# Gated linear attention and a channel mixer on one core: batch 0 by token slot, more transposes by DMA, and a new written-out order

## The chip, the cores and the metric

The kernel runs on one core of a Trainium2 chip. A core has a matrix engine (PE, with its weight load PEld), a vector engine (DVE), an activation engine (ACT), a general engine (POOL), and a queue engine (SP) that issues transfers; ACT can issue transfers too. All of them run their own list of instructions strictly in order and meet at semaphores. Sixteen DMA engines move the data. The metric is device time in microseconds (us), the median of several runs.

## The reference, cut to what matters

```
state = zeros(B, H, D, D)                       # B=4, H=8, D=48, S=768 tokens
for t in range(S):
    state = alpha[t][:, None] * state + outer(k[t], v[t])
    y[t] = q[t] @ state
x  = y as (B, S, H*D)                            # H*D = 384
h  = relu(x^T @ w_tok1) @ w_tok2                 # 768 -> 256 -> 768, over tokens
u  = x + h^T
out = u + relu(u @ w_ch1) @ w_ch2                # 384 -> 1536 -> 384, over channels
```

The recurrence is computed in chunks: cumulative products of alpha (as exponentials of cumulative sums of logarithms) scale k and q, a masked product of scaled q and k gives the part within a chunk, and a carried state gives the rest. Everything in and out is float32; the matrix work is in bf16.

## The kernel before, in words

**Attention.** Twelve units n = 0 to 11, three to a batch of 256 tokens each. A unit loads alpha, k, q and v (`ld_at`, `ld_kt`, `ld_qt`, `ld_vt`, 384 KB each, L534). A partition holds two neighbouring tokens, its two slots. In the wide units, 0 to 2 (batch 0), logarithms (`ln`), cumulative sums by matrix product (`cumw`, L608) and exponentials (`E`, `IE`, `Et`) cover both slots; the others fold the two slots first (`P`, `k0a`, `q0r`). `kk` and `qq` scale k and q (L640), and eight transposes on PE for each (`trk`, `trq`) with an eviction (`evk`, `evq`) turn them; from unit 6 on, DMA transposes issued by SP do it (`dk`, `dq`, L664) with a reorder of q behind (`pq`). `G0`, `G1` are the products within a half of the unit, `mask0`, `mask1` the masked evictions on DVE (L700). Six half-tile copies (`vs0`, `vs1`, `ka`, `kb`, `kc`) regroup v and k so that `K`, the update of the state, runs on full 128-row tiles. The states follow as an add on DVE (`sa`) and a multiply (`sm`). `y0`, `y1` with `ia`, `ib` give the outputs and `x0`, `x1` evict them.

**Mixer.** For each batch b: `t1_b` (token matrix 1, L787), its rectifying evictions `ht_b`, `t2_b` (L792), `u_b` (add on DVE, L796, six tiles), the transposes of u, `c1_b` (channel matrix 1, 24 groups of three 128x384 products, L811) with evictions `rt_b` on ACT or DVE, `c2_b` (six rows of four groups, L816), `o_b` (add on DVE, L820) and a store `st_b` (L574). The transposes of u are `up` on PE with evictions `ut` in batches 0 and 1, and `ux`, a DMA transpose on SP, in batches 2 and 3. PE's results lie in eight PSUM banks. The output tiles `o` are three: an `o` waits until the store of the earlier content of its tile has landed.

**Order.** Nothing is scheduled on the chip or by the compiler. `ORDER` lists every step with its engine's letter (t PE, s ACT, v DVE, g POOL, y SP), `BUFS` the buffer of every tile; a search outside the kernel wrote both. Steps of one engine run in the listed order. Loads and weight pieces are issued by SP and ACT. [...] `f1`, `f3` steps are fillers: PE products of zeros that keep it busy at the start.

Of the kernel before, what the change touches and what calls it, by code (L numbers as in the profile page):

```python
# [110 lines left out]
WIDE = (0, 1, 2)  # L111

# [3 lines left out]
def build(g):  # L116
# [8 lines left out]
    def filler(nm, bank):  # L125
        return [P.op(f"f{z}_{nm}", {"PE": pe([512] * z)["PE"], "NONE": (0.0, 0.0)}, -100, writes=[bank],
                     emit=lambda e, z=z: g.fill(bank, z)) for z in (1, 3)]

    def attention(n):
# [8 lines left out]
        def fill(nm, bank):  # L138
            return filler(f"{nm}{n}", bank) if n < NB else []

        at, kt, qt, vt = V("in"), V("in"), V("in"), V("in")
# [4 lines left out]
        la, E, IE = V("la"), V("E"), V("IE")
        pkk, pkq, vb = V("pkk"), V("pkq"), V("vb")
        k_in, q_in = [ld["kt"]], [ld["qt"]]
        if n in WIDE:
# [4 lines left out]
            e1 = O("E", act(768), 4, writes=[E], reads=[cb], preds=[cum], emit=lambda e: g.exps(E, cb, 1.0))
            et = O("Et", act(16), 6, writes=[E], reads=[cb], preds=[cum], emit=lambda e: g.exptot(E, cb))
            e2 = O("IE", act(768), 3, writes=[IE], reads=[cb], preds=[cum], emit=lambda e: g.exps(IE, cb, -1.0))
        else:
# [8 lines left out]
            e1 = et = O("E", act(400), 4, writes=[E], reads=[cb], preds=[cum], emit=lambda e: g.expE(E, cb))  # L166
            e2 = O("IE", act(384), 4, writes=[IE], reads=[cb], preds=[cum], emit=lambda e: g.expIE(IE, cb))
# [5 lines left out]
        kk = O("kk", either(dve(768), pool_tt(768)), 5, writes=[pkk], reads=[kt, IE], port=True, preds=k_in + [e2],  # L173
               emit=lambda e: g.scaled(e, pkk, kt, IE, wide))
        qq = O("qq", either(dve(768), pool_tt(768)), 5, writes=[pkq], reads=[qt, E], port=True, preds=q_in + [e1],
               emit=lambda e: g.scaled(e, pkq, qt, E, wide))
# [3 lines left out]
        if n < NX:  # L180
            bk, bq = V("one"), V("one")
            trk = O("trk", pe([128] * 8), 8, writes=[bk], reads=[pkk], preds=[kk] + fill("trk", bk),
                    emit=lambda e: g.trw(bk, pkk))
            evk = O("evk", either(dve(1024, True), act(1024)), 9, writes=[tpk], reads=[bk], preds=[trk],
                    emit=lambda e: g.trwev(e, tpk, bk))
            trq = O("trq", pe([128] * 8), 8, writes=[bq], reads=[pkq], preds=[qq] + fill("trq", bq),
                    emit=lambda e: g.trw(bq, pkq))
            evq = O("evq", either(dve(1024 * 1.065), act(1024 * 1.34)), 9, writes=[tpq], reads=[bq], preds=[trq],
                    emit=lambda e: g.qev(e, tpq, g.bank(bq).bitcast(BF16)))
        else:  # L190
            evk = O("dk", {"SP": (1240.0, 1240.0)}, 9, writes=[tpk], reads=[pkk], preds=[kk],
                    emit=lambda e: g.xbar(tpk, pkk), dma=("x", 1400.0, 1180.0, 480.0))
            tqx = V("tpk")
            xq = O("dq", {"SP": (1240.0, 1240.0)}, 9, writes=[tqx], reads=[pkq], preds=[qq],
                   emit=lambda e: g.xbar(tqx, pkq), dma=("x", 1400.0, 1180.0, 480.0))
            evq = O("pq", either(dve(1024), act(1024 * 1.35, True), {"POOL": (1100.0, 1140.0)}), 9.5, port=True, writes=[tpq], reads=[tqx], preds=[xq],
                    emit=lambda e: g.qev(e, tpq, g.t(tqx)))
        gtm = V("gtm")
        masks = []
        for hf in range(2):  # L200
            gp = V("pair")
            G = O(f"G{hf}_", pe([128] * 4), 10 + hf, writes=[gp], reads=[tpk, tpq], preds=[evk, evq] + fill(f"G{hf}", gp),
                  emit=lambda e, hf=hf, gp=gp: g.gmm(gp, tpk, tpq, hf), mode="G")
            masks.append(O(f"mask{hf}_", dve(1024), 12 + hf, writes=[gtm], reads=[gp], preds=[G],
                           emit=lambda e, hf=hf, gp=gp: g.mask(gtm, gp, hf)))
        nst = 2 if k < NB - 1 else 1
        kp = V("pair")
# [4 lines left out]
        vsw = lambda hf, preds: shift(f"vs{hf}_", 10, [vb], [vt], preds, lambda e: g.vswap(e, vb, vt, hf))  # L212
        turned = n >= KFN
        if turned:
            vs = [vsw(hf, [vc]) for hf in range(2)]
            kx, kp_in = None, [kk, vc, vs[0]]
            if nst == 2:
                kx = V("kt")
                ka = shift("ka", 9, [kx], [pkk], [kk], lambda e: g.kturn(e, kx, pkk, 0))
                kb = shift("kb", 9, [kx], [pkk], [kk], lambda e: g.kturn(e, kx, pkk, 1))  # L220
                kp_in += [ka, kb, vs[1]]
            kc = shift("kc", 9, [pkk], [], [kk, trk if n < NX else evk] + ([ka] if nst == 2 else []),
# [4 lines left out]
        else:  # L227
            KO = O("K", {"PE": (276.0 if nst == 2 else 140.0, 420.0)}, 9.5, writes=[kp], reads=[pkk, vb],
                   preds=[kk, vc] + fill("K", kp) + ([prev_s[1]] if prev_s and k > 0 and n > NB else []),
                   emit=lambda e: g.kmm(kp, pkk, vb, nst), mode="G")  # L230
            vs = [vsw(hf, [KO, vc]) for hf in range(2)]
        before = prev_s if k > 0 else None
        states = [before]
        for hf in range(nst):
            s_, sp = V("ss"), states[-1]
            if sp is None:
                so = O(f"s{hf}_", dve(384), 10, writes=[s_], reads=[kp, E], preds=[KO, et],
                       emit=lambda e, s_=s_, hf=hf: g.sfirst(s_, kp, E, hf, wide, turned))
            else:
                t_ = V("tmp")  # L240
                ad = O(f"sa{hf}_", dve(384), 10 + hf, writes=[t_], reads=[kp, sp[0]], preds=[KO, sp[1]],
                       emit=lambda e, t_=t_, hf=hf, s0=sp[0]: g.sadd(t_, kp, s0, hf, turned))
                so = O(f"sm{hf}_", either(dve(384), pool_tt(384)), 11 + hf, writes=[s_], reads=[t_, E], port=True,
                       preds=[ad, et], emit=lambda e, s_=s_, t_=t_, hf=hf: g.smul(e, s_, t_, E, hf, wide))
            states.append((s_, so))
        for hf, st in enumerate(states[:2]):
            yp, x = V("one"), V("x")
            held = []
            if st:
                held.append(O(f"i{'ab'[hf]}", pe([96] * 4), 13, writes=[yp], reads=[tpq, st[0]],  # L250
                              preds=[evq, st[1]] + (fill("y", yp) if hf else []),
                              emit=lambda e, hf=hf, st=st, yp=yp: g.inter(yp, tpq, st[0], hf)))
            yo = O(f"y{hf}_", pe([48] * 8), 14, writes=[yp], reads=[gtm, vb],
                   preds=[masks[hf], vs[hf]] + held,
                   emit=lambda e, hf=hf, yp=yp, st=st: g.ymm(yp, gtm, vb, hf, not st))
# [619 lines left out]
```

## Time and profile before

| | |
|---|---|
| runs | 167.32, 166.66, 166.67 us; median 166.67 |
| profiled execution | span 165.0 us from first to last instruction; its whole time isn't given on the page, the median lies 1.67 us above its span |
| busy | PE 156.2 us (95%), DVE 121.2 (73%), ACT 96.2 (58%), POOL 68.7 (42%) |
| granted PE clock | 1.000 over the span |
| first product of c1_0 / last PE product | starts 37.34 us / ends 161.97 us |

A row of a group reads: line, engine, operation, output<-input, shapes, count, then busy us and mean ns of one, then the idle time of the engine ahead of it and what ended that. A row of the timeline reads: start us, length us, engine, line, operation, count. A row of the stretches reads: from:to, length, and for each engine its busy us with the count, then the granted clock, the busy share of the DMA engines and GB/s.

### The profile page before, as it was taken

The numbers are of one execution on the slowest core, as the hardware profiler recorded it, in microseconds if no ns is written. First come the engines' busy times: TensorE is split into PE (matmuls) and PEld (weight loads), VectorE is DVE, ScalarE is ACT, GpSimd is POOL, SyncE is SP. The second block draws the span as 40 slices with busy tenths as digits, with TensorE's granted clock in tenths as the row PEclk, the third lists the DMA queues.
The fourth block names the chain that finished last, engine by engine and source line by source line (L and its number), as shares of the span: only waits on it lengthen the run. The fifth ranks groups of instructions, "written<-read, shape, count | busy, mean of one in ns | idle before, by whom it ended". The sixth has DMA issues, their size and how long they took to land.

```text
span 165.0 us, 4235 instructions
## 1 busy us (share of the span) xinstructions
PE 156.2 (95%) x1683; PEld 99.2 (60%) x1683; DVE 121.2 (73%) x210; ACT 96.2 (58%) x186; POOL 68.7 (42%) x84
## 2 busy tenths in 40 slices
PE   7969769999999999999999999999999999999992
PEld 2435446666666766576666666666666656656662
DVE  4098989989898898798878999989492455524422
ACT  3599987998877837939887746913614001514110
POOL 4025659497217475792388528973300000000000
PEclk9999999999999999999999999999999999999999
DMA  4999999999999999999989996898001136200213
GB/s 121 324 325 325 337 347 316 365 327 352 371 335 347 326 315 226 307 252 264 136 198 255 211 250 120 219 181 183 0 4 48 49 75 157 105 0 0 99 72 119
DMA packets 74531, 34.48 MB, mean 209 GB/s; under 512 B 67984, under 2 KB 73488, under 8 KB 74512
## 3 DMA queue, kind: packets, MB, share of 16 engines
q1 hardware_dynamic: 50576, 23.30, 55.2%
q10 hardware_dynamic: 23936, 10.91, 24.3%
q8 instruction: 13, 0.21, 0.5%
q14 instruction: 6, 0.05, 0.1%
HBM read 25.17 MB, written 4.72 MB: 181 GB/s over the span
## 4 chain that ended last, share of the span: by engine, by line
PE 83%; DMA 4%; SPq 3%; POOL 2%; issue 2%; ACT 2%; DVE 1%; POOLq 0%; DVEq 0%
PE ps L816 29%; PE ps L811 29%; PE ps L593 14%; PE ps L792 5%; DMA in<-in_v_dram 4%; PE ps L787 4%; SPq L534 3%; PE ps L654 1%; PE ps L803 1%; POOL pkk L642 1%; DVE gtm L700 1%; POOL vb L685 1%; ACT x L684 1%; POOL ss L753 1%; ACT E L626 0%
## 5 line engine op out<-in xcount | busy, mean ns | idle before, releaser
L816 PE MATMUL ps<-wc,rt 128*128 128x384 bf16 (+1 forms) x300 | 54.7, 320 | 0.0
L811 PE MATMUL ps<-ut,wc 128*128 128x384 bf16 x288 | 51.3, 326 | 0.0
L782 ACT ACTIVATE rt<-ps 128x384 bf16<-128x384 f32 x54 | 24.4, 490 | 35.4 <-PE ps L811 34.7
L811 PEld LDWEIGHTS <-wc 128*128 128x128 bf16 x288 | 27.1, 98 | 16.7
L816 PEld LDWEIGHTS <-rt 128*128 128x128 bf16 x300 | 27.5, 98 | 15.9
L700 DVE TENSOR_TENSOR gtm<-ps,mk 128x1024 bf16<-128x1024 f32 x24 | 28.7, 1219 | 4.8 <-PE ps L593 3.4
L784 DVE TENSOR_SCALAR rt<-ps 128x384 bf16<-128x384 f32 x42 | 21.7, 551 | 9.2 <-PE ps L811 9.2
L820 DVE TENSOR_TENSOR o<-ps,u 128x384 f32<-128x384 f32 (+1 forms) x25 | 13.1, 537 | 10.0 <-PE ps L816 9.1
L685 POOL CAST vb<-in 64x384 bf16<-64x384 f32 (+1 forms) x18 | 10.9, 608 | 15.2 <-DVE pkk L642 8.9
L593 PE MATMUL ps<-zs 128*128 128x512 bf16 x38 | 12.7, 452 | 2.9 <-DVE zs L496 1.1
L684 ACT CAST x<-ps 128x384 bf16<-128x384 f32 x17 | 7.8, 477 | 10.7 <-PE ps L593 10.5
L796 DVE TENSOR_TENSOR u<-ps,x 128x384 bf16<-128x384 f32 x24 | 11.8, 550 | 3.0 <-PE ps L792 3.0
L642 DVE TENSOR_TENSOR pkq<-in,E 128x768 bf16<-128x768 f32 x8 | 7.6, 954 | 5.4 <-ACT E L626 5.2
L787 PE MATMUL ps<-x,wt 128*128 128x384 bf16 x48 | 11.1, 325 | 0.5 <-DVE gtm L700 0.4
L684 ACT CAST vb<-in 64x384 bf16<-64x384 f32 (+1 forms) x18 | 11.1, 618 | 0.7 <-DMA in<-in_v_dram 0.2
L642 POOL TENSOR_TENSOR pkk<-in,IE 128x768 bf16<-128x768 f32 x5 | 9.1, 1816 | 4.9 <-DVE pkk L685 3.2
L753 POOL TENSOR_TENSOR ss<-tmp,E 128x384 bf16<-128x384 f32 x11 | 9.2, 833 | 3.2 <-DVE tmp L750 2.9
L750 DVE TENSOR_TENSOR tmp<-ps,ss 128x384 f32<-128x384 f32 x16 | 8.8, 552 | 1.0 <-PE ps L593 0.5
L792 PE MATMUL ps<-ht,wt 128*128 128x384 bf16 x48 | 9.5, 326 | 0.0
L593 PEld LDWEIGHTS <-gtm 128*128 128x128 bf16 x192 | 7.4, 96 | 2.7 <-DVE gtm L700 0.9
L593 PEld LDWEIGHTS <-tpk 48*64 48x64 bf16 x384 | 6.1, 106 | 4.9 <-issue 4.3
L593 PE MATMUL ps<-vb,gtm 128*128 128x48 bf16 x192 | 8.6, 183 | 0.4 <-DVE gtm L700 0.4
(91 smaller groups left out, 216.6 us busy)
## 6 DMA issues: line engine op xcount, KB each, us to landing
in<-in_moe_w_ch_dram SPq DMA_DIRECT2D x10, 384.0 KB, 6.2
in<-in_alpha_dram SPq DMA_DIRECT2D x9, 384.0 KB, 6.8
out_dram<-o SPq DMA_DIRECT2D x16, 192.0 KB, 2.5
in<-in_q_dram SPq DMA_DIRECT2D x7, 384.0 KB, 6.3
in<-in_v_dram ACTq DMA_DIRECT2D x7, 384.0 KB, 6.0
in<-in_k_dram ACTq DMA_DIRECT2D x6, 384.0 KB, 5.7
in<-in_k_dram SPq DMA_DIRECT2D x6, 384.0 KB, 6.2
in<-in_v_dram SPq DMA_DIRECT2D x5, 384.0 KB, 7.2
```

The costliest lines, as they stand in the source:

```text
L593: return self.pe.matmul(out, lhsT=lhsT, rhs=rhs, start=start, stop=stop, skip_group_check=True)
L642: self.shared(self.eng[e].tensor_tensor(self.t(dst)[:, :, :, 0:D], self.t(src).rearrange("p h s d -> p s h d"), bass.AP(tensor=f.tensor, o ...
L684: return self.act.copy(d, s)
L685: return self.shared(self.eng[e].tensor_copy(d, s))
L700: self.nc.vector.tensor_tensor(self.t(gtm)[:, hf, :, :], self.pair(gp).rearrange("p a (j t) -> p (a j) t", t=128), bass.AP(tensor=m.tensor ...
L782: self.act.activation(d, s, AF.Relu)
L784: self.nc.vector.tensor_scalar_max(d, s, 0.0)
L787: self.pe.matmul(self.bank(bank)[:, 0:HD], lhsT=self.wt1[:, kc, m * 128 : m * 128 + 128], rhs=self.t(x), start=(kc == 0), stop=(kc == NS - 1))
L792: self.pe.matmul(self.bank(bank)[:, 0:HD], lhsT=self.wt2[:, kc, i * 128 : i * 128 + 128], rhs=self.t(hts[kc]), start=(kc == 0), stop=(kc = ...
L811: self.pe.matmul(self.bank(bank)[:, 0:HD], lhsT=self.wc1[:, kc, mc * 128 : mc * 128 + 128], rhs=self.t(ut)[:, 3 * half : 3 * half + 3, kc, ...
L816: self.pe.matmul(self.bank(bank)[:, 0 : cz - ca], lhsT=self.t(rts[mc][0])[:, i * 128 : i * 128 + 128], rhs=self.wc2[:, mc, ca:cz], start=( ...
L820: self.nc.vector.tensor_tensor(self.t(o)[:, ca:cz], self.bank(bank)[:, 0 : cz - ca], self.t(u)[:, i % 3, ca:cz], ALU.add)
```

## The change

- **Batch 0 (units 0 to 2) by token slot.** `gslot` puts the two halves of a unit on the partitions and gives one tile to each slot, with a new mask `mkw` (`maskslot`). `K` becomes `khalf`: 16 (unit 2: 8) products on 64-row tiles instead of 8 (4) on 128 rows. `y` becomes one step `yslot` of 32 products on 64-row tiles instead of two of 8. The copies `vs`, `ka`, `kb`, `kc` of these units go. The old state is added on PE (`A`, `kadd`, one 128x384 product), so `sa` and `sm` become one `s` on DVE. `Et` goes: the totals come with `E`, now 800 wide.
- **u of batch 1 by DMA.** `UP` is (0,), so `up_1` (18 PE transposes) and `ut_1` (three evictions) give way to `ux_1_0` and `ux_1_1` on SP.
- **Queues.** All loads and weights are issued by SP (`LOADQ`), none by ACT. Most stores go to ACT. The weight pieces 0 to 2 of `w_ch1` are cut by 256 columns over all three row blocks.
- **Fillers** come as counts of 1 to 12 ahead of any PE step of batch 0.
- **ORDER and BUFS are new throughout.** The places the prediction speaks of:

```diff
-UP = (0, 1)
+UP = (0,)
+LOADQ = ({"SP": (420.0, 420.0)}, {"SP": (420.0, 420.0)})
...
+            kps = [V("one") for _ in range(nst)]
+            K = O("K", {"PE": (430.0, 560.0)}, 9.5, writes=kps, reads=[pkk, vb], preds=kk + [vc],
+                  emit=lambda e, first=before is None: g.khalf(kps, pkk, vb, first), mode="Y")
+            for hf in range(nst):
+                kp, s_, sp = kps[hf], V("ss"), states[-1]
+                KO = K
+                if sp is not None:
+                    KO = O(f"A{hf}_", pe([384]), 9.6 + hf, writes=[kp], reads=[sp[0]], preds=[K, sp[1]],
+                           emit=lambda e, kp=kp, s0=sp[0]: g.kadd(kp, s0))
+                so = O(f"s{hf}_", dve(384), 10 + hf, writes=[s_], reads=[kp, E], preds=[KO, et],
+                       emit=lambda e, s_=s_, kp=kp, hf=hf: g.sfirst(s_, kp, E, hf, wide))
...
+ld_at0y ld_at1y ln0s f8_cumw0t f1_cumw0t cumw0t IE0s ld_kt0y kk0g ln1s f6_cumw1t f1_cumw1t cumw1t ld_vt0y vb0s K0t E0s
...
+c2_0_2_2t c2_0_2_3t kb6s ux_1_0y c2_0_0_3t c1_1_11_0t rt_1_11_0s st_0_3s u_1_3v st_0_5s st_0_1s u_1_4v ux_1_1y q0r7g
+c1_1_4_0t rt_1_4_0s ka6v c2_0_4_2t qq6g o_0_0v st_0_0s c1_1_5_0t o_0_2v vs1_6v c1_1_3_0t cum7t IE7s E7s c1_1_8_0t
...
+u_2_2v ld_qt10y dq9y pq9g cum10t E10s t2_2_0t u_2_0v c2_1_0_2t dk9y c2_1_5_0t c2_1_5_1t c2_1_5_2t ux_2_1y q0r10v kc9s
...
+st_3_1y o_3_4v c2_3_0h0_1t c2_3_3_2t c2_3_3_3t c2_3_0h0_2t o_3_3v c2_3_0h0_3t st_3_4s o_3_0h0v st_3_0h0s st_3_3s
```

By engine and in `ORDER`'s sequence, around the start of c1_1: ACT has `rt_1_11_0 st_0_3 st_0_5 st_0_1 rt_1_4_0 st_0_0 IE7 E7`; DVE has `u_1_4 ka6 o_0_0 o_0_2 vs1_6 kk7 qq7 o_0_4`; PE has `c1_1_11_0 c1_1_4_0 c2_0_4_2 c1_1_5_0 c1_1_3_0 cum7 c1_1_8_0`. `o_0_5`, `o_0_1`, `o_0_3` hold the three output tiles 0, 1, 2; `o_0_0` takes tile 0, `o_0_2` tile 1. By `BUFS`, `c1_1_3_0` takes the bank that `rt_1_4_0` empties and `cum7` the bank that `o_0_2` empties.

More of the change, by code (lines that the diff above doesn't have):

```diff
@@ L122, in build, with fillers @@
     pools = {}
-    def filler(nm, bank):
-        return [P.op(f"f{z}_{nm}", {"PE": pe([512] * z)["PE"], "NONE": (0.0, 0.0)}, -100, writes=[bank],
-                     emit=lambda e, z=z: g.fill(bank, z)) for z in (1, 3)]
+    def fillers():
+        for o in list(P.ops):
+            nm = o.name
+            if "PE" in o.eng and (nm[:4] in ("t1_0", "t2_0", "up_0") or nm.split("_")[-1][-1] in "0123" and nm[:2] not in ("t1", "t2", "up", "c1", "c2") and not nm.endswith("10") and not nm.endswith("11")):
+                bank = V("one")
+                for z in (1, 2, 3, 4, 6, 8, 12):
+                    P.op(f"f{z}_{nm}", {"PE": pe([512] * z)["PE"]}, -100, writes=[bank],
+                         emit=lambda e, z=z, bank=bank: g.fill(bank, z))
     def attention(n):
@@ L172, in attention @@
         wide = n in WIDE
[L173 to L176, printed above, removed]
+        kk, qq = [], []
+        for zi, (z, h0, h1) in enumerate(parts):
+            w = (h1 - h0) * 2 * D
+            kk.append(O(f"kk{z}", either(dve(w), pool_tt(w)), 5, writes=[pkk], reads=[kt, IE], port=True,
+                        preds=(k_in if len(parts) == 1 else [k_in[zi]]) + [e2[zi]],
+                        emit=lambda e, h0=h0, h1=h1: g.scaled(e, pkk, kt, IE, wide, HD, h0, h1)))
+            qq.append(O(f"qq{z}", either(dve(w), pool_tt(w)), 5, writes=[pkq], reads=[qt, E], port=True, preds=q_in + [e1[zi]],
+                        emit=lambda e, h0=h0, h1=h1: g.scaled(e, pkq, qt, E, wide, 400, h0, h1)))
         vc = O("vb", either(dve(768, True), pool_cp(768), act(768, True)), 7, writes=[vb], reads=[vt], port=True,
@@ L201, in attention @@
             gp = V("pair")
[L202 to L203 removed]
+            G = O(f"G{hf}_", pe([128] * 4), 10 + hf, writes=[gp], reads=[tpk, tpq], preds=[evk, evq],
+                  emit=lambda e, hf=hf, gp=gp: (g.gslot if wide else g.gmm)(gp, tpk, tpq, hf), mode="G")
             masks.append(O(f"mask{hf}_", dve(1024), 12 + hf, writes=[gtm], reads=[gp], preds=[G],
[L205 removed]
+                           emit=lambda e, hf=hf, gp=gp: (g.maskslot if wide else g.mask)(gtm, gp, hf)))
         nst = 2 if k < NB - 1 else 1
[L207 removed]
         def shift(nm, i, writes, reads, preds, fn):
@@ L226, in attention @@
                    emit=lambda e: g.kfull(kp, pkk, kx, vb, nst))
[L227 to L245, printed above, removed]
+            for hf in range(nst):
+                s_, sp = V("ss"), states[-1]
+                if sp is None:
+                    so = O(f"s{hf}_", dve(384), 10, writes=[s_], reads=[kp, E], preds=[KO, et],
+                           emit=lambda e, s_=s_, hf=hf: g.sfirst(s_, kp, E, hf, wide, hf))
+                else:
+                    t_ = V("tmp")
+                    ad = O(f"sa{hf}_", dve(384), 10 + hf, writes=[t_], reads=[kp, sp[0]], preds=[KO, sp[1]],
+                           emit=lambda e, t_=t_, hf=hf, s0=sp[0]: g.sadd(t_, kp, s0, hf))
+                    so = O(f"sm{hf}_", either(dve(384), pool_tt(384)), 11 + hf, writes=[s_], reads=[t_, E], port=True,
+                           preds=[ad, et], emit=lambda e, s_=s_, t_=t_, hf=hf: g.smul(e, s_, t_, E, hf, wide))
+                states.append((s_, so))
+        yps, helds, xts = [], [], []
         for hf, st in enumerate(states[:2]):
@@ L358, in build @@
         mixer(b)
+    fillers()
     return P
```

372 lines of the change are left out of this document (214 added, 158 removed), and 22 rows, old and new, of the table BUFS.

## The prediction

> **What bounds the kernel now.** I read the page first, then the busy times by stretch, with cuts where the mixer's products begin to run (31.4, 37.34) and where PE ends (161.97).
>
> ```profile
> span 165.0 us, 4235 instructions
> PE 156.2 (95%) x1683; PEld 99.2 (60%) x1683; DVE 121.2 (73%) x210; ACT 96.2 (58%) x186; POOL 68.7 (42%) x84
> PE   7969769999999999999999999999999999999992
> PEclk9999999999999999999999999999999999999999
> GB/s 121 324 325 325 337 347 316 365 327 352 371 335 347 326 315 226 307 252 264 136 198 255 211 250 120 219 181 183 0 4 48 49 75 157 105 0 0 99 72 119
> ```
> ```profile
> 0.00:16.00 16.00, 13.43 (x125) 6.86 (x126) 8.65 (x25) 11.03 (x16) 4.94 (x17) 1.00 0.99 273
> 16.00:31.40 15.40, 12.32 (x219) 8.30 (x217) 14.34 (x20) 13.48 (x26) 9.94 (x13) 1.00 1.09 338
> 31.40:37.34 5.94, 5.94 (x90) 4.29 (x90) 5.33 (x11) 5.55 (x10) 5.66 (x7) 1.00 1.10 339
> 37.34:161.97 124.63, 124.55 (x1257) 79.74 (x1254) 92.54 (x156) 66.12 (x137) 48.14 (x49) 1.00 0.73 180
> 161.97:164.96 2.99, 0.00 (x0) 0.00 (x0) 0.36 (x1) 0.00 (x0) 0.00 (x0) 1.00 0.45 161
> ```
>
> The fourth stretch decides the case: from the first product of c1_0 PE is busy 124.55 of 124.63 us. The time is therefore three terms: when c1_0 starts (37.34), how much PE work is left then, and the tail behind PE (2.99). A change gains only by starting c1_0 earlier or by having less PE work behind it; every wait of PE behind that point is added whole. Ahead of it DVE is the fullest (14.34 of 15.40 us), with the loads at 325 to 338 GB/s.
>
> **Start.** Where PE and DVE stand in the old start, in order of time, and groups by shape:
>
> ```profile
> 5.00 1.58 ACT L587 ACTIVATE la<-in 128x768 bf16<-128x768 f32 x2 [2.92 <-DMA in<-in_alpha_dram]
> 6.62 0.65 PE L593 MATMUL ps<-la,u 128*128 128x384 bf16 x3
> 7.68 0.81 ACT L626 ACTIVATE E<-ps 128x768 f32<-128x768 f32 x1 [1.10 <-PE ps L593]
> 8.39 0.81 ACT L626 ACTIVATE IE<-ps 128x768 f32<-128x768 f32 x1
> 13.19 1.22 DVE L700 TENSOR_TENSOR gtm<-ps,mk 128x1024 bf16<-128x1024 f32 x1 [0.53 <-PE ps L593]
> 23.15 2.35 DVE L700 TENSOR_TENSOR gtm<-ps,mk 128x1024 bf16<-128x1024 f32 x2
> 33.49 2.88 DVE L796 TENSOR_TENSOR u<-ps,x 128x384 bf16<-128x384 f32 x6 [0.33 <-PE ps L792]
> 37.34 2.64 PE L811 MATMUL ps<-ut,wc 128*128 128x384 bf16 x15
> ```
> ```profile
> L700 DVE TENSOR_TENSOR gtm<-ps,mk 128x1024 bf16<-128x1024 f32 x24 | 28.7, 1219 | 4.8 <-PE ps L593 3.4 <-ACT lf L590 1.0
> L782 ACT ACTIVATE rt<-ps 128x384 bf16<-128x384 f32 x54 | 24.4, 490 | 35.4 <-PE ps L811 34.7 <-DVE o L820 0.4
> L820 DVE TENSOR_TENSOR o<-ps,u 128x384 f32<-128x384 f32 x23 | 12.4, 552 | 7.8 <-PE ps L816 6.9 <-PE ps L811 0.9
> L642 POOL TENSOR_TENSOR pkk<-in,IE 128x768 bf16<-128x768 f32 x5 | 9.1, 1816 | 4.9 <-DVE pkk L685 3.2 <-DVE pkk L642 1.1 <-POOL in L634 0.5
> L642 DVE TENSOR_TENSOR pkk<-in,IE 128x768 bf16<-128x768 f32 x7 | 6.7, 954 | 1.1 <-POOL vb L685 0.6 <-issue 0.3
> L684 ACT COPY tpq<-ps 128x1024 bf16<-128x1024 bf16 x3 | 4.0, 1317 | 0.2 <-PE ps L654 0.2
> L685 DVE COPY tpk<-ps 128x1024 bf16<-128x1024 bf16 x4 | 2.6, 683 | 0.0
> ```
>
> Removed for batch 0: the `vs`, `ka`, `kb`, `kc` copies, four `sa` (their state add is now `s`, which also replaces `sm`), `Et`, and on ACT all load issues. What is left is the chain of DVE. Its first mask comes later than before: one load alone lands about 0.7 us ahead of the 5.00 above, where two share the engines (384 KB at 325 GB/s is 1.2 us, less the slow first half us). From 4.3: `ln0` 0.84, `cumw0` 1.06 (6.62 to 7.68), `IE0` 0.81, end 7.05; `kk0` is now on POOL, 1.82, end 8.9; then PE has K0 and trk0 (1.1) and six fillers (1.3) ahead of `cumw2` (1.06), 12.4; `IE2` and `E2` on ACT at 0.71 each (7.68 to 8.39), 13.8; `evq0` on ACT 1.32, 15.2; `A1_0` and three fillers 0.8, `G0_0` 0.4: `mask0_0` starts at 16.4, not 13.19.
>
> From there DVE's list to the last `ut_0` is: six masks at 1.22 (7.3), four `s` at 0.55 (2.2), `kk2` and `qq3` (1.9), `evk2` 0.7, `evq2` 1.3, four 384-wide ones (2.2), `vs0_3` 0.3, six `u` (2.9), two `ut` (1.1): 19.8 us, less 0.05 of overlap for each of 20 neighbours (two masks take 2.35, not 2.44), plus 1.25 of waits that nothing hides (`y2` behind the last mask 0.65, `trk2` 0.3, `up_0_0` 0.3): 20.1. So c1_0 starts at 36.5: **-0.84**. The removed steps' whole worth lies in this term; the loads in SP's new order (27 of them to `w_ch1`'s pieces, 1.1 to 1.2 us apart) and POOL's `cw_wc13` end at 33 to 37 and are just hidden. Bounds: 35.4 if the 1.25 of waits vanish, 37.6 if POOL's chain (`k0a4`, `kk4`, `kb4`, `cw_wc13`, each in its turn behind `qq3`) ends last.
>
> **PE work behind that.** From the chain of waits and the DMA issues:
>
> ```profile
> 72.19 0.34 PE ps L803 x6
> 72.87 3.90 PE ps L811 x24
> ```
> ```profile
> in<-in_alpha_dram SPq DMA_DIRECT2D x9, 384.0 KB, 6.8
> out_dram<-o ACTq DMA_DIRECT2D x7, 192.0 KB, 2.2
> tpk<-pkq SPq DMA_TRANSPOSE x6, 4.5
> out_dram<-o SPq DMA_DIRECT2D x1, 96.0 KB, 1.6
> ut<-u SPq DMA_TRANSPOSE x4, 3.2
> ```
> ```profile
> L574 ACTq DMA_DIRECT2D out_dram<-o x8: 338/338/363, 62.4 to 159.0; - x8
> DMA to landing us min/median/max: 1.6/2.2/5.4
> ```
>
> Three times six transposes go with `up_1`: 3 x 0.34 = **-1.02**. `trk4` moves ahead of c1_0 while `cum5` and `ib3` move behind it, which is even. The batch-0 parts (64-row K and y, the four `A`) lie ahead of c1_0, in PE's idle time there, and cost nothing but what the chain above has. `ux_1_0` is safe: between the end of `t2_1_0` and `c1_1_11_0` PE has 5.7 us of products listed, and an `u` (0.6) and a transpose (3.2) fit, so I cost it at nothing; at 5.3 us landing it would be 0.2 late.
>
> **New waits behind c1_0.** (a) c1_0's first evictions come behind `mask1_3`, `mask0_3` on DVE (2.4) and `cw_wc14`, `cw_wc10`, `evk4`, `ka4`, `lnP5` on ACT; with eight banks PE stands **+0.4** in short pieces (0 to 1.5).
>
> (b) The start of c1_1. Let it be C. A group of three products takes 0.49 (24 in 3.90). `o_0_5`, `o_0_1`, `o_0_3` fill all three output tiles, and their stores are listed on ACT behind `rt_1_11_0`, the eviction of c1_1's first group. That ends at C+0.49+0.12+0.49 = C+1.1; the three issues (0.34 each, 0.40 apart) begin at 1.15, 1.55, 1.95; at 2.2 to landing the second is done at 3.75 and the third at 4.15. `o_0_0` wants the second's tile: 3.8 to 4.35. `o_0_2` wants the third's: 4.35 to 4.9. `cum7` wants the bank `o_0_2` empties: C+4.95. Without the wait PE would be there after five groups, at C+2.45. So PE stands **+2.5**, 0.9 of it earlier (`c1_1_3_0` needs `rt_1_4_0`, which queues on ACT behind the same three issues). Behind the waiting `o_0_0` on DVE stand `o_0_2`, `kk7`, `qq7`, `o_0_4`; behind `st_0_0` on ACT, which waits for `o_0_0`, stand `IE7`, `E7` and four evictions. In the old trace DVE's waits ahead of an output add are for PE alone (the L820 row), so there this wait has no counterpart. Bounds: landing 1.6 makes it 1.9; 5.4 makes it 5.7.
>
> [...]
>
> (c) The start of c1_2. `ux_2_1` is listed on SP behind `dq9` and `dk9`, and `dk9` waits for `kk9` on POOL, behind a list of `sm`, `q0r`, `P`, `k0a` at 0.8 to 1.0 and `qq9`, `kk9` at 1.8; `pq9` is as late, and `G1_9` needs it. POOL's sum from `kc7` to `kk9` is 14.5 us plus its waits for `sa1_7` and `dq8`, and it ends about where PE asks. I take **+0.6**; 0 if POOL is early, +2.7 if a transpose lands in 5.3 instead of 3.2 there.
>
> **Tail.** The last store was 96 KB, alone, landing in 1.6. Now `st_3_3` (192 KB) is issued on ACT behind `st_3_0h0`: one issue later (0.38) and some 0.3 longer under way: **+0.7** (0.4 to 1.0).
>
> **Sum.** -0.84 - 1.02 + 0.4 + 2.5 + 0.6 + 0.7 = +2.3 on the profiled execution: span 167.3 for 165.0. The median of the runs stands 1.67 above that span; with the same around it the time is 166.67 + 2.3 = **169.0 us**.
>
> **Rivals.**
> - *The hold at c1_1 isn't there*, because something the list doesn't show lets the tiles free sooner or C waits for `ux_1_0` anyway. For it: PE had no wait at all in the old stretch, so such lists can be good. Against: the order on ACT, DVE and PE is fixed, and the tiles are three. 169.0 - 2.5 = 166.5, no change.
> - *The start gains enough* (the faster side): one mechanism, DVE's shorter list ahead of c1_0. Its price is 1 us for each us that c1_0 starts earlier; with everything else as above it must start before 36.5 - 3.2 = 33.3 for a gain of 0.5%. For it: DVE loses some 3 us of adds and scalings. Against: `mask0_0` starts three us later, and `w_ch1`'s pieces land only at some 32 (24 loads at 1.2 behind the one at 4.3, the weights a little faster) and must be cast, 0.83. At that bound, 32.9, the time is 169.0 - 3.6 = 165.4.
> - *Transposes land late.* SP carries all loads and 18 transposes, and `dk`, `dq` landed in 4.5 to 5.3 where `ux` took 3.2. If `ux_2` takes 5.3 as well, (c) is 2.7: 171.1.
> - *PE's clock falls in the hold.* Its 2.5 us come as 0.9 and 1.6. The old row of granted clock shows full speed also in slices where PE was busy for 6 or 7 tenths. If the seven groups behind the hold ran at half speed, that is 7 x 0.49 = 3.4 more: 172.4. [...]
>
> **How the numbers follow.** Forecast 0.50, no hold 0.18, the start 0.12, late transposes 0.16, clock 0.04. Half a per cent, 0.83 us, is about what a measurement of this kernel can tell from no change. The start case is faster, and 0.02 of the no-hold case: 0.14. The rest of no-hold is the same: 0.16. The others are slower: 0.70. The range runs from the no-hold case to the late transposes, 166.3 to 171.2; the start case and the upper end (0.06) are left out. The forecast's own range, with (b) 1.9 to 3.2 and the start 35.9 to 37.1, is 167.8 to 170.3.
>
> **What would show it.** First product of c1_0 at 36.5 (35.4 to 37.6), no L803 transposes of batch 1; PE idle 0.9 and 1.6 us within 5 us of the first c1_1 product (at some 69.5 us, 32.5 us of listed PE work behind c1_0's first), with DVE's L820 add ended by a store's landing; ACT idle ahead of `st_0_0`; a tail of 3.7 us behind PE's last product; the granted clock 1.00. Wrong would be: PE busy throughout at c1_1, c1_0 ahead of 35, or PE idle of over a us at a place not named here.

## The result, and the profile after

The changed kernel takes 174.81 us (median of 174.75, 177.02, 174.87, 174.52) against 166.71 for the kernel before, on the same chip: a ratio of 1.0498, interval 1.0436 to 1.0560. Slower was right; 169.0 was 5.8 us too little, and the time lies outside the range. Medians are over all executions of a kernel; the ratios and their intervals leave out executions more than 1.5% above the kernel's fastest, and the profiled ones of e2_busy and e4_all are among these, so their places are used beside those of another kernel.

The profiled execution took 174.75, its span is 173.0. From its page, busy times and the rows in 40 slices:

```profile
span 173.0 us, 4340 instructions
PE 159.8 (92%) x1742; PEld 100.7 (58%) x1742; DVE 113.1 (65%) x198; ACT 93.7 (54%) x179; POOL 75.7 (44%) x85
PE   7999959979999999957999999969999999999991
PEclk9999995699999999999999999999999999999999
```

And the stretches that answer to those of before (from:to, length, busy us of PE, PEld, DVE, ACT, POOL, granted clock, DMA share, GB/s):

```profile
16.00:22.64 6.64, 6.47 (x142) 4.21 (x136) 6.01 (x8) 4.12 (x7) 2.54 (x2) 1.00 1.07 287
22.64:26.05 3.41, 1.53 (x36) 0.74 (x34) 3.41 (x4) 2.12 (x5) 3.33 (x4) 1.00 1.09 347
26.05:32.88 6.83, 6.83 (x114) 4.68 (x114) 2.70 (x4) 3.77 (x9) 3.86 (x6) 0.50 1.02 329
32.88:40.79 7.91, 6.99 (x101) 4.90 (x99) 7.23 (x14) 7.01 (x12) 4.43 (x5) 1.00 1.07 324
40.79:169.19 128.40, 124.05 (x1245) 78.86 (x1238) 86.77 (x142) 66.27 (x138) 56.66 (x57) 1.00 0.73 175
169.19:173.00 3.81, 0.00 (x0) 0.00 (x0) 0.39 (x2) 0.00 (x0) 0.00 (x0) 0.98 0.30 107
```

c1_0 starts at 40.79, not at 36.5. PE's granted clock is 0.50 from 26.05 to 32.88; DVE, the engine that the prediction's start was counted on, is busy for only 2.70 of those 6.83 us. Behind c1_0, PE stands for 4.35 us (128.40 less 124.05); before it was 0.08. Its waits, and DVE's for stores (us in total, times, longest):

```profile
PE ps L646 <- DVE o L899: 2.2, 1, 2.2
PE ps L890 <- DMA ut<-u: 1.4, 1, 1.4
PE ps L890 <- ACT rt L861: 0.6, 1, 0.6
DVE o L899 <- DMA out_dram<-o: 5.8, 3, 3.6
```

The chain that ended last, at the start of c1_1 (product, eviction, ACT's issue of the first two stores, the third store from its issue to its landing, `o_0_2`, `cum7`) and of c1_2 (landing of `ux_2_0`, products):

```profile
73.47 0.50 PE ps L890 x3
73.99 0.02 ACT rt L861
74.05 0.38 ACTq L627
74.47 0.44 ACTq L627
74.95 3.24 DMA out_dram<-o
78.28 0.57 DVE o L899
78.90 0.43 PE ps L646 x6
...
109.57 5.25 DMA ut<-u
114.86 8.45 PE ps L890 x51
```

Term by term, in us of the two profiled executions (their spans differ by 8.04):

| term | predicted | measured | from |
|---|---|---|---|
| start of c1_0 | -0.84 | +3.45 | 37.34 to 40.79 |
| PE work behind it | -1.02 | -0.50 | 124.55 to 124.05 |
| (a) first evictions | +0.4 | 0 | PE busy from 40.79 to 73.30 |
| (b) hold at c1_1 | +2.5 | +2.8 | 2.2 + 0.6 |
| (c) start of c1_2 | +0.6 | +1.4 | 1.4 |
| tail | +0.7 | +0.8 | 3.00 to 3.81 |

The small rest is idle time in pieces. 4.3 of the 5.7 us missed are the start. The experiments therefore ask three things: is it the clock that moved the start, are the stores the hold, and why do some transposes land late.

### The profile page after: what moved, and what is told of

Same layout as the page of the kernel before. It is cut to its first block, busy times and chain, and to the rows that moved or that the text cites. A ratio compares the mean times of both kernels' runs of the same rounds, so it can differ in the third digit from the quotient of the medians.

```text
span 173.0 us, 4340 instructions
## 1 busy us (share of the span) xinstructions
PE 159.8 (92%) x1742; PEld 100.7 (58%) x1742; DVE 113.1 (65%) x198; ACT 93.7 (54%) x179; POOL 75.7 (44%) x85
## 4 chain that ended last, share of the span: by engine, by line
PE 63%; DMA 15%; ACT 9%; POOL 5%; issue 2%; DVE 2%; SPq 1%; ACTq 1%; POOLq 0%; DVEq 0%
PE ps L890 23%; PE ps L895 22%; PE ps L646 10%; DMA tpk<-pkk 4%; PE ps L866 3%; DMA in<-in_k_dram 3%; DMA ut<-u 3%; DMA in<-in_v_dram 3%; PE ps L871 3%; POOL pkk L700 2%; DMA out_dram<-o 2%; PE ps L712 2%; DVE u L875 1%; SPq L581 1%; ACT E L683 1%
## 5 line engine op out<-in xcount | busy, mean ns | idle before, releaser
L895 PE MATMUL ps<-wc,rt 128*128 128x384 bf16 (+1 forms) x300 | 53.9, 320 | 0.2 <-ACT x L742 0.2
L890 PE MATMUL ps<-ut,wc 128*128 128x384 bf16 x288 | 51.6, 326 | 2.0 <-DMA ut<-u 1.4
L890 PEld LDWEIGHTS <-wc 128*128 128x128 bf16 x288 | 26.9, 97 | 18.8 <-issue 2.2
L758 DVE TENSOR_TENSOR gtm<-ps,mk 128x1024 bf16<-128x1024 f32 x18 | 21.4, 1219 | 3.0 <-PE ps L646 2.4
L742 ACT CAST x<-ps 128x384 bf16<-128x384 f32 x20 | 9.3, 478 | 14.0 <-PE ps L646 13.8
L700 POOL TENSOR_TENSOR pkk<-in,IE 128x768 bf16<-128x768 f32 x8 | 14.5, 1818 | 4.9 <-ACT IE L687 4.6
L646 PE MATMUL ps<-rt 128*128 128x512 bf16 x40 | 12.7, 449 | 1.1 <-DVE rt L538 1.1
L692 POOL TENSOR_TENSOR in<-in,in 128x384 f32<-128x384 f32 x7 | 7.0, 997 | 13.9 <-PE ps L871 5.7
L631 POOL TENSOR_TENSOR in<-in 128x384 f32<-128x384 f32 x9 | 9.0, 999 | 8.3 <-DMA in<-in_alpha_dram 5.0
L696 POOL TENSOR_TENSOR in<-in,lf 128x384 f32<-128x384 f32 x7 | 7.0, 996 | 9.1 <-ACT lf L643 3.3
L646 PE MATMUL ps<-tpq,tpk 48*64 48x128 bf16 x384 | 9.0, 224 | 0.9 <-DVE gtm L774 0.7
L743 POOL CAST vb<-in 128x768 bf16<-128x768 f32 (+1 forms) x10 | 7.0, 696 | 5.3 <-DVE pkq L700 3.0
```

The lines of the kernel that those rows point to most:

```text
L646: return self.pe.matmul(out, lhsT=lhsT, rhs=rhs, start=start, stop=stop, skip_group_check=True)
L700: self.shared(self.eng[e].tensor_tensor(self.t(dst)[:, :, h0:h1, 0:D], self.t(src)[:, h0:h1].rearrange("p h s d -> p s h d"), bass.AP(tens ...
L742: return self.act.copy(d, s)
L758: self.nc.vector.tensor_tensor(self.t(gtm)[:, hf, :, :], self.pair(gp).rearrange("p a (j t) -> p (a j) t", t=128), bass.AP(tensor=m.tensor ...
L890: self.pe.matmul(self.bank(bank)[:, 0:HD], lhsT=self.wc1[:, kc, mc * 128 : mc * 128 + 128], rhs=self.t(ut)[:, 3 * half : 3 * half + 3, kc, ...
L895: self.pe.matmul(self.bank(bank)[:, 0 : cz - ca], lhsT=self.t(rts[mc][0])[:, i * 128 : i * 128 + 128], rhs=self.wc2[:, mc, ca:cz], start=( ...
```

## The experiments

Twelve kernels ran beside the kernel before, whose median was then 167.3 to 167.4. Times are compared by their ratios to it, places by the profiles. An edit can shift the line numbers: the products of c1 (L890) stand at L891 in e2_busy and e3_half1.

**e1_stores: the three stores earlier on ACT.**

```diff
-rt_1_11_0s st_0_3s u_1_3v st_0_5s st_0_1s u_1_4v
+rt_1_11_0s u_1_3v u_1_4v
+... st_0_5s E6s ... st_0_1s st_0_3s kb6s ...
```

> The changed kernel with three stores issued earlier on ACT: st_0_5 ahead of E6, st_0_1 and st_0_3 ahead of kb6, all ahead of c1_1's first eviction. Theory (the hold): the 2.2 and 0.6 us that PE stands at the start of c1_1 come from the landings of these stores alone, 3.2 us after the issue at 74.95. Then the output adds wait for PE only, PE has under 0.5 us of idle time in the 6 us behind c1_1's first product, and the time falls by 2.3 to 2.8, to 172.0 to 172.5. Rival: the tiles are one of two locks, and the second transpose of u or the evictions queued on ACT hold PE next: the time falls by under 1.2.

170.80 us, ratio 1.0223 (1.0175 to 1.0271). The chain at the same place (start, length in us, what it is):

```profile
73.67 0.97 PE ps L890 x6
74.64 0.49 PE ps L895 x3
75.13 0.97 PE ps L890 x6
76.11 0.27 PE ps L646 x6
```

DVE's remaining wait for a store (us in total, times, longest):

```profile
DVE o L899 <- DMA out_dram<-o: 1.5, 1, 1.5
```

PE runs through: idle from c1_1's to c1_2's first product falls from 2.98 to 0.24 us, though c1_0 starts where it did (40.99). `cum7` starts 2.4 us behind c1_1's first product instead of 5.6. The hold was these stores, as (b) says. The profiled span is 3.1 us shorter (169.9); the whole time gains more, some 4.6 us by the ratios. The mean granted clock of its other three executions was 0.990 to 1.000, against 0.971 to 0.980 in all four of the changed kernel, so part of the gain is the clock's.

**e2_busy: the same order, PE busier at 23 to 25 us.** `G0_1` and `G0_2` run twice over the same results.

```diff
-emit=lambda e, hf=hf, gp=gp: (g.gslot if wide else g.gmm)(gp, tpk, tpq, hf), mode="G")
+emit=lambda e, hf=hf, gp=gp: [(g.gslot if wide else g.gmm)(gp, tpk, tpq, hf)
+                              for _ in range(2 if n in (1, 2) and hf == 0 else 1)], mode="G")
```

> The changed kernel with the products of G0_1 and of G0_2 issued twice each (the second time over the same results), which puts some 0.84 us more of PE work into the stretch 22.6 to 26.0, where PE was busy 1.53 of 3.41 us; the order and all else stay. Theory W (the clock): PE's granted clock fell to 0.50 for 6.83 us because of that thin stretch, and the 6.83 us of products at half speed are what makes c1_0 late. Then the clock is 1.00 throughout, c1_0's first product starts some 3.4 us earlier, at 37.5 (up to 38.5 if a cast or a landing ends last instead), and the time is 171.3 to 172.4. Rival L (the chain): c1_0 is late because the k tile of attention step 3 lands at 21.8 and POOL, ACT and the weight casts follow it; PE's half speed is hidden behind them. Then the clock may be 1.00 but c1_0 starts within 0.8 us of 40.9 and the time is 174 to 175. Rival D: the clock falls anyway, the products being too few, and nothing changes.

174.88 us, ratio 1.0433 (1.0374 to 1.0491): no gain that can be told. But its stretches, and the group of the weight loads of c1's products, whose row gives ns of one (least, median, longest) and the times of the first and the last, say where it went:

```profile
22.60:26.00 3.40, 2.38 (x75) 1.52 (x74) 3.40 (x4) 2.51 (x6) 3.38 (x3) 1.00 1.10 351
26.00:32.80 6.80, 6.12 (x130) 4.07 (x126) 4.91 (x9) 5.87 (x13) 3.54 (x6) 1.00 0.94 289
```
```profile
L891 PEld LDWEIGHTS <-wc x288: 95/98/151, 38.3 to 165.0; 128*128 128x128 bf16 x144
```

PE is busy 2.38 us of the stretch instead of 1.53, the clock holds, and c1_0 starts at 38.3: 2.5 us earlier for 0.85 us of work that computes nothing. So theory W holds for the start; of 3.4 us, 2.5 came, since something else ends last at 38.3 (g2_loads and h1_kt3 below start at 38.44 and 38.47). The gain was then lost at c1_1: here the stores landed 5.9 us behind their issue, PE stood 4.9 us for `cum7`, and the clock fell there. The next kernel's profile shows such a fall too.

**e3_half1: two products of c1_2 that don't need `ux_2_0` moved ahead.**

```diff
-G0_9t mask0_9v c1_2_2_0t c1_2_9_1t ... c1_2_2_1t
+G0_9t mask0_9v c1_2_9_1t c1_2_2_1t c1_2_2_0t ...
```

> The changed kernel with two products of c1_2 that need only the first of the two transposed halves (c1_2_9_1, c1_2_2_1) moved ahead of the first that needs the second (c1_2_2_0). Theory: PE stands 1.37 us at c1_2 for the landing of ux_2_0, 2.5 us behind that of ux_2_1 on the one queue, and two groups at 0.49 cover 0.98 of it: time 173.7 to 173.9. Rival: an eviction or a bank ends last there, and the time stays within 0.3 of 174.8.

175.07 us, ratio 1.0498 (1.0450 to 1.0546): no gain in the time. `c1_2_2_1` now waits for the bank that `mask0_9` empties, as the rival has it: 0.9 us are left of the 1.4. The whole time doesn't measure this edit alone, because in this profile the clock fell at other places. PE's wait there, and four stretches of 3.4 us:

```profile
PE ps L891 <- DVE gtm L759: 0.9, 1, 0.9
```
```profile
22.69:26.10 3.41, 1.60 (x41) 0.95 (x40) 3.41 (x4) 2.18 (x6) 3.33 (x4) 1.00 1.11 362
26.10:29.52 3.42, 3.42 (x66) 2.50 (x64) 2.16 (x4) 1.68 (x4) 2.84 (x6) 0.50 1.10 332
73.89:77.30 3.41, 0.65 (x3) 0.29 (x3) 0.56 (x2) 0.48 (x1) 0.00 (x0) 1.00 0.95 253
77.30:80.72 3.42, 2.81 (x14) 1.44 (x14) 2.28 (x4) 0.89 (x2) 0.99 (x1) 0.50 1.04 229
```

The clock falls twice, each time for one window of 3.41 us right behind a window in which PE did little. The second is the rival that the prediction gave 0.04, in this kernel and not in the changed one's profile; PE was busy for 0.65 us of the window ahead of it, and for 1.60 of the one ahead of the fall at the start.

This profile also measures the start again, with nothing changed ahead of it: with one window at half speed instead of two, c1_0 starts at 39.22. With two it was 40.79 and 40.99 (e1_stores), with none 38.3 (e2_busy): each window costs 0.9 to 1.8 us.

**e4_all: the three edits together, and `st_3_3` ahead of `st_3_0h0`.**

```diff
-st_3_4s o_3_0h0v st_3_0h0s st_3_3s
+st_3_4s st_3_3s o_3_0h0v st_3_0h0s
```

> The edits of the three runs before together, and the store st_3_3 issued ahead of st_3_0h0 on ACT. If the terms add up: 174.8 - 2.6 (stores) - 3.3 (clock) - 1.0 (half) - 0.4 (tail) = 167.5, c1_0 at 37.5, PE without a wait of over 0.5 us behind it. If the waits hide each other or the chain L holds c1_0: 169.5 to 171.5.

171.20 us (168.69 to 171.78), ratio 1.0163 (1.0096 to 1.0229). The executions spread over 3 us, all but one at a mean granted clock of 1.00, so something besides the clock varies between them; what it is stays open. In the profile c1_0 is at 38.2, the clock at 1.00, the tail 3.3 instead of 3.8. The terms didn't add up: PE stood 1.4 us for `ux_1_0`, 1.2 for `dk9`, and 0.9 at c1_2 for the bank that `mask0_9` empties. `ux_1_0` landed 6.0 us behind its issue and `dk9` 5.6, where the changed kernel had 3.0 and 2.7. The order on SP is the same. What differs is where the trace's instruction queue fetches program code: with `dk9` under way it moved 0.02 MB between 102 and 104.5 us in e4_all, and nothing between 106.5 and 108 in the changed kernel. Theory F: a DMA transpose lands late when such a fetch falls behind its issue. The next runs test that.

**g1_shift: PE's program longer from the start** (on e4_all). 64 tiny products stand for five of eight fillers.

```diff
+        if count == 8:
+            count = 3
+            for _ in range(64):
+                self.mm(self.bank(bank)[0:64, 0:48], self.zs[:, 0:64], self.zs[:, 0:48], True, True)
```

> The kernel e4_all, with 64 tiny products (64 rows out, 48 columns) in place of five of the eight 512-wide fillers ahead of the first cumulative sum: PE's program is some 120 instructions longer from there on, and nothing else changes. [...] Shifted, the fetch at 67.5 goes to some 59 and the one at 103.7 to some 97, out of ux_1_0 and dk9: ux_1_0 lands in 3.0 to 4.4 instead of 6.0, dk9 in 2.7 instead of 5.6, PE's waits for them (1.36 and 1.17 us) go, and the time falls by 1.5 to 2.5 from e4_all's 171.2. Rival Q (queue): they land late behind loads and other transposes on the one SP queue; then the landings and the time stay within 0.5 of e4_all.

170.04 us, ratio 1.0162 (1.0130 to 1.0193). From c1_0's first product (39.70) to PE's end:

```profile
39.70:165.17 125.47, 124.06 (x1245) 78.95 (x1238) 86.78 (x142) 66.19 (x138) 56.78 (x57) 1.00 0.72 184
```

PE's waits at c1_1 are gone and 0.15 is left at `G1_9`. For the same stretch e4_all needs 128.04 us (38.20 to 166.24) and h1_kt3, whose lists are the same there, 126.86 (38.47 to 165.33). `ux_1_0` landed after 4.1, `dk9` after 2.7, as theory F has it. The whole time didn't fall as expected: the ratios of e4_all and g1_shift are the same (1.0163 and 1.0162), c1_0 starting 1.5 us later. The clearest pair is the last transpose of batch 3's u, beside which its queue has nothing but the end of the transpose ahead of it. First h1_kt3 (below) from 140.5 to 143, then the changed kernel from 144.3 to 146; the last figure is us from issue to landing:

```profile
q8 instruction: 1, 0.02, 2.6%
ut<-u SPq DMA_TRANSPOSE x1, 4.3
```
```profile
q1 hardware_dynamic: 222, 0.05, 13.5%
ut<-u SPq DMA_TRANSPOSE x1, 2.8
```

The same pair for `dk9`, h1_kt3 from 101.7 to 103.1 and the changed kernel from 106.5 to 108:

```profile
q8 instruction: 1, 0.02, 8.0%
tpk<-pkk SPq DMA_TRANSPOSE x1, 4.8
```
```profile
q1 hardware_dynamic: 832, 0.20, 61.2%
tpk<-pkk SPq DMA_TRANSPOSE x1, 2.7
```

Over the changed kernel and its eleven variants, `dk9` and that last transpose landed in 2.7 to 2.8 us wherever no such fetch fell between issue and landing (seven kernels each, `dk9` of h3_best with 2.7 and the last transpose of g1_shift with 2.8 among them), and in 4.3 to 5.6 wherever one did (five each, e4_all with 5.6 and 4.4 among them). The steps just ahead of them on SP are the same in all, so theory Q doesn't explain these two.

**g2_loads: two loads from ahead of `ux_1_0` to behind `ux_1_1`** (on e4_all).

```diff
-... vb6g ld_at9y IE6s ... lnP8s ld_at10y cum8t ... ux_1_0y ... ux_1_1y
+... vb6g IE6s ... lnP8s cum8t ... ux_1_0y ... ux_1_1y ld_at10y ld_at9y
```

> The kernel e4_all, with the loads ld_at9 and ld_at10 moved on SP from ahead of ux_1_0 to behind ux_1_1. Theory Q: ux_1_0 lands late because two loads of 1.2 us stand ahead of it in the queue; it then lands in under 4 us, PE's 1.36 us at c1_1 go and the time falls by 1.0 to 1.4. Theory F: the fetches at 67.5 and 68.5 still hit it; it lands 5 us or more after its issue and the time stays within 0.5 of e4_all.

172.11 us, ratio 1.0285 (1.0247 to 1.0323), slower than e4_all. `ux_1_0` landed in 3.0 us (issues from 66 to 67) and its wait at c1_1 went, which is what theory Q expected:

```profile
ut<-u SPq DMA_TRANSPOSE x1, 3.0
```

But the 16 KB fetch came at 65.9 here, ahead of the issue at 66.43, so theory F doesn't expect a late landing either: for `ux_1_0` the run doesn't tell the two apart. PE's idle time between c1_1 and c1_2 rose to 3.9 us, it seems because the two loads now come later, and that took the gain away.

**g3_dve: `evq2` and `vs0_3` from DVE to ACT** (on e4_all).

```diff
-x1_0s ... evq2v ... vs0_3v trk3t kc3s
+evq2s x1_0s ... trk3t vs0_3s kc3s
```

> The kernel e4_all, with evq2 (1.31 us on DVE) and vs0_3 (0.35) moved from DVE to ACT, where ACT had nothing to do at 20.5 and 27.3. If DVE's list sets c1_0's start when the clock holds (in e4_all DVE is busy 19.3 of the 21.5 us from mask0_0 to the last ut_0), c1_0 comes 1.0 to 1.7 earlier, at 36.5 to 37.2 instead of 38.2. If PE or the loads set it, c1_0 stays within 0.4 of 38.2. PE's thin stretch comes earlier and may make the clock fall again, which would cost up to 3.4.

171.20 us, ratio 1.0244 (1.0191 to 1.0297). Inconclusive on DVE's list: the thinner stretch let the clock fall for one window (27.00 to 30.41), and c1_0 started at 39.33.

**g4_sum: g1_shift, g2_loads and g3_dve together, without e3_half1's edit.**

> The edits of g1_shift, g2_loads and g3_dve together, on e4_all without its reordering of c1_2 (which gained nothing in e3_half1). If they add up: c1_0 at 37, PE idle behind it under 1.5 us, span 165 to 166.5, time 166.5 to 168.5, level with the kernel before. If a fetch hits another transpose or the clock falls: 169 to 172.

172.20 us, ratio 1.0274 (1.0236 to 1.0312): g2_loads' idle time again (3.3 us between c1_1 and c1_2), c1_0 at 39.13.

**h1_kt3: the chain of step 3's k tile shortened** (on e4_all).

```diff
-ld_qt2y ld_kt2y ld_vt2y ld_kt3y          cw_wt10g E3s t1_0_0_0t P4g vb3g K2t kb3g ... vs1_3g vs0_3v trk3t kc3s
+ld_qt2y ld_kt3y ld_kt2y ld_vt2y          kb3g cw_wt10g E3s t1_0_0_0t vb3g K2t ... vs1_3g P4g trk3t vs0_3s kc3s
```

> The kernel e4_all, with the load of step 3's k tile moved two places forward in SP's queue, kb3 ahead of cw_wt10 and P4 behind vs1_3 on POOL, and vs0_3 on ACT instead of DVE. Theory: once the clock holds, c1_0 follows the landing of that tile through POOL's list (k0a3, kk3, casts, vb3), vs0_3, mask1_2 and y2: in e2_busy, e4_all and g1_shift the tile landed at 21.41, 21.29 and 22.80 and c1_0 started 16.9 later each time. With the tile at 19 to 20, POOL starts when qq2 ends (19.55) and c1_0 comes 0.8 to 1.5 earlier, at 36.7 to 37.4. Rival: DVE's or PE's own list sets it (36.5 was the prediction's sum for DVE) or ACT's cw_wt20 ahead of ht_0_0, and c1_0 stays within 0.4 of 38.2.

170.40 us, ratio 1.0167 (1.0118 to 1.0216); c1_0 at 38.47. The tile landed at 18.65 instead of 21.29 and c1_0 didn't move: the chain that ended last now came from `kt2`, over DVE's `evq2` and masks and ACT's `cw_wt20`, `lnP4`, `ht_0_0`. The theory falls as the one cause; with the clock held, several lists seem to end together near 38.2.

**h3_best: h1_kt3 without e3_half1's edit, and the fetches shifted by two later fillers as 36 tiny products each.**

> The edits of h1_kt3 on the changed kernel with the earlier stores, the doubled products and the tail's store, without the reordering of c1_2, and with two fillers (f4_K1, f3_trq2) as 36 tiny products each, which moves PE's program fetches some 130 instructions earlier without touching the first loads as g1_shift did. If all hold: c1_0 at 37, ux_1_0, dk9 and ux_2 landing without a 16 KB fetch behind their issue, PE idle behind c1_0 under 1 us, span 164.5 to 165.5, time 166.3 to 167.3, level with the kernel before. If a fetch hits a transpose again: 168 to 169.5. If the tiny products are too little work and the clock falls: 169 to 171.

169.87 us, ratio 1.0164 (1.0116 to 1.0212). The fetch theory holds a second time: `ux_1_0` landed after 3.1, `dk9` after 2.7, and PE needed 125.70 us from c1_0 (38.91) to its end. 1.3 us of idle time are left from c1_2 on, and c1_0 isn't at 37.

**h4_best: h3_best with `evq2` to ACT, `cw_wt20` to POOL, `lnP4` behind `ht_0_1`.**

```diff
-x1_0s ... evq2v ... cw_wt11g ... cw_wt20s lnP4s ... ht_0_0s ht_0_1s
+evq2s x1_0s ... cw_wt11g cw_wt20g ... ht_0_0s ht_0_1s lnP4s
```

> The kernel h3_best, with three more steps moved off the lists that end together at c1_0's start: evq2 from DVE to ACT, cw_wt20 from ACT to POOL, and lnP4 behind ht_0_1 on ACT. If those lists (DVE's masks, ACT's last casts) set c1_0, it comes 0.5 to 1.2 us earlier than h3_best's 38.91 and the time is 168.7 to 169.5; if PE's own products set it, it stays within 0.3. If the thinner stretch lets the clock fall: 170.5 to 172.

170.04 us, ratio 1.0158 (1.0116 to 1.0200), c1_0 at 39.24. What was moved made new waits of PE:

```profile
PE ps L871 <- POOL wt L748: 1.1, 1, 1.1
PE ps L647 <- ACT la L638: 1.0, 1, 1.0
```

**b1_fill: the kernel before with seven more fillers where PE was idle.**

```diff
-f1_cumw2t   -trq2t            -f1_y2t
+f3_cumw2t   +f3_trq2t trq2t   +f3_y2t
```

> The kernel before, with seven more 512-wide fillers (products that compute nothing) in three places where PE stood idle anyway: two ahead of G0_0 (idle 0.88 us at 11.5), three ahead of trq2 (0.85 at 19.7), two ahead of the filler of y1_1 (0.99 at 22.5). Theory W: the old kernel, too, has thin stretches, and in the executions whose mean granted clock is 0.99 one window of 3.4 us ran at half speed; they took 167.1 to 168.5 where those at 1.00 took 166.3 to 167.1. With the added work the clock is 1.00 in all of them and the median falls from 167.4 to 166.3 to 166.9, though PE does more. Rival: the 0.99 comes from elsewhere, or work that computes nothing delays the rest: the median stays at 167.4 or rises by up to 0.6.

166.58 us (12 executions, 166.46 to 167.19) against 167.41 (17 executions): ratio 0.9963, interval 0.9938 to 0.9988. It is the fastest kernel here. Its mean granted clock was 0.998 to 1.000 in all twelve. Of the old kernel's seventeen, twelve had 0.99 and took 167.15 to 168.88, five had 1.00 and took 166.34 to 166.70. One window of 3.41 us at half speed in a span of 165.5 makes a mean of 0.99.

```profile
core 0: 164.8 us, clock 1.000
```

So 1.5 us more of PE work (seven fillers, which start 0.215 us apart at 8.4 us in the profile of the kernel before) made the kernel faster by 0.4%, by taking that fall out: against the five executions without it nothing is gained. Theory W holds for the old kernel too. Its profile is of an execution without the fall, which is why the prediction saw none.

## Why the prediction was right and wrong

- **Direction.** Right, and the hold at c1_1 alone would have given it. But the largest term was forecast as a gain: the start came 3.45 us late instead of 0.84 early. Of the costs named behind c1_0, (b), (c) and the tail came, (a) didn't.
- **Start, -0.84: the step that failed.** `mask0_0` started at 16.39, as summed, though the chain to it ran over the load of v and ACT (`vb0`, `E0`, `E1`, `IE1`, `ln2`) and not over POOL's `kk0`, so the agreement is in part luck. From there the prediction counted DVE's list and put PE's new 64-row parts in "PE's idle time there". It took this work to cost nothing and didn't ask what the remaining idle time does to PE's clock: it weighed the clock only for the hold, and read full speed from 40 slices of 4.1 us, longer than the 3.41 us for which the clock fell in e3_half1. PE was busy 1.53 us of the window 22.64 to 26.05 and then ran 6.83 us at half speed. e2_busy gives 2.5 us of the 4.3 missed to that. The other 1.8 (38.3 against 36.5) are waits that the list of DVE didn't contain: 1.25 us were allowed for them, and with the clock held DVE's stretch from `mask0_0` to the last `ut_0` was 21.5 us instead of 20.1. Which list sets 38.2 isn't settled: shortening one (h1_kt3, h4_best) let another end last, and g3_dve was spoilt by the clock. The bounds 35.4 to 37.6 came from one engine's list and were too narrow. The rival of the falling clock (172.4) took seven groups at half speed, a term that the trace of before doesn't show; the clock held at the hold of the changed kernel, and stood at 0.50 there for 6.83 us in e2_busy and 3.42 in e3_half1.
- **PE work behind, -1.02.** The eighteen transposes went, but the exchange called "even" wasn't. Groups of the stretch behind c1_0, after and then before:

```profile
L646 PE MATMUL ps<-ss,tpq 128*128 128x96 bf16 x60 | 5.0, 207 | 0.0
L646 PE MATMUL ps<-la,u 128*128 128x384 bf16 x7 | 2.3, 325 | 2.2 <-DVE o L899 2.2
```
```profile
L593 PE MATMUL ps<-ss,tpq 128*128 128x96 bf16 x56 | 4.5, 206 | 0.0
L593 PE MATMUL ps<-la,u 128*128 128x384 bf16 x6 | 2.0, 326 | 0.0
```

  `ib3` adds 0.5 and `cum5` 0.3 with more in its small products; `trk4`, eight transposes, took 0.6 away.
- **(a), +0.4.** Wrong by its size: PE was busy throughout.
- **(b), +2.5.** Right in mechanism, place and size: 0.6 us for `rt_1_4_0` and 2.2 for `cum7`, which came 5.6 us behind c1_1's first product where 4.95 was summed. The last landing took 3.24 us instead of the 2.2 used. Transposes and a load were under way beside it, and what made it longer wasn't tested. The first two landed in 2.36 and 2.47. The rival without a hold was refuted by PE's waits, and e1_stores shows their cause.
- **(c), +0.6.** Right place, too small: 1.4 of the 2.7 allowed. The order of issue was as named: `dk9` went out at 106.83, when POOL ended `kk9`, and `ux_2_1` and `ux_2_0` behind it. `dq9` and `dk9` landed in 2.7 us; what was late were `ux_2_1` and `ux_2_0`, with 4.2 and 5.3, as the rival of late transposes has it. At 3.2 `ux_2_0` would have landed at 112.8, ahead of PE's need at 113.5. Code fetches fell behind the issue of both; that they are the cause isn't shown for these two.
- **"`ux_1_0` is safe".** True in the changed kernel (3.0 us), and no longer in e4_all (6.0). The margin summed allowed for a landing in 5.1; by the trace it was 4.5 (landed 71.75, needed at 73.30).
- **Tail, +0.7.** Right: 0.8, and e4_all took 0.5 of it back.

## What to carry to other kernels

Idle time of an engine that isn't the bound can cost: six times in these profiles PE's granted clock fell to 0.50, each time behind a stretch of 3.41 us in which PE was busy for only 0.65 to 2.08 us. So look at what PE does in stretches of that length, not in the page's slices, and try filling thin ones with products that compute nothing: with 2.38 us busy instead of 1.53 the clock held in e2_busy. One profile without a fall doesn't mean that there is none; compare the granted clock of all executions. A store that is issued late holds its tile for the issue queue and the landing (at c1_1 two issues of 0.38 and 0.44 us ahead of the third store, then 3.24 us), so list it as soon as its data is ready.

## What the runs showed of the hardware

**Where the granted clock fell.** Between the first and the last product it fell six times, for 6.83 us (the changed kernel, e1_stores, e2_busy) or 3.41 (twice in e3_half1, g3_dve), at places that differ from profile to profile. At 1.00 the fillers of the changed kernel start 0.215 us apart (22.47 us), at 0.50 they start 0.427 apart (30.98). PE was busy for 1.53, 2.08, 1.32, 1.60, 0.65 and 2.03 us of the 3.41 us ahead of these falls; in the window ahead of 26.05 no idle piece was longer than 1.0 us, and PE was busy 45% of it. The busy share alone doesn't sort the windows. First the changed kernel, whose clock held behind the first of these windows and stayed at half behind the second, in which PE was busy throughout; then e1_stores, whose clock fell behind a window with more than the first:

```profile
77.25:80.66 3.41, 1.76 (x16) 1.11 (x16) 1.60 (x4) 0.89 (x2) 1.00 (x1) 1.00 1.22 208
26.05:29.46 3.41, 3.41 (x67) 2.67 (x67) 2.07 (x4) 1.53 (x4) 2.83 (x5) 0.50 1.07 337
```
```profile
22.94:26.35 3.41, 2.08 (x49) 1.16 (x42) 3.41 (x4) 2.67 (x6) 3.33 (x4) 1.00 1.09 353
26.35:33.18 6.83, 6.83 (x114) 4.68 (x114) 3.21 (x5) 3.79 (x8) 3.78 (x6) 0.50 1.00 319
```

The window that held has 11 products of 384 columns on full 128x128 weights among its 16; of the 36 in the changed kernel's window ahead of its fall (22.64 to 26.05), 32 are small (48x64 weights, 128 columns). So the size of the products may count beside the busy time, but no run varied it alone, and what decides isn't shown.

**Transposes with a code fetch behind their issue landed later.** The changed kernel's page has 13 fetches of together 0.21 MB, 16 KB each, for 3,484 PE rows: on average one per 268. Longer PE programs moved them (g1_shift, h3_best: between 100 and 110 us e4_all has one of 16 KB and h3_best none). The two transposes compared above landed 1.5 to 2.9 us later with one behind their issue. PE itself shows no loss by them: it was busy throughout from 40.79 to 73.30, with three fetches of 16 KB in between (53.4, 60.4 and 72.8 us). Why the transposes wait, and how much the smaller fetches of 8 KB on a second instruction queue do, stays open.
